# One issue order of a scheduled SSM-and-MLP kernel replaced by another

## Chip, cores and metric

The kernel runs on one core of a Trainium2 chip. The metric is the device time of one execution in microseconds; 153.26 us is the median of three runs of the kernel before (153.21 to 153.65). The engines are named as the profile names them: PE is TensorE (matmuls), PEld its weight loads, DVE is VectorE, ACT is ScalarE, POOL is GpSimd, SP is SyncE, which here only issues transfers. Each engine takes its own instructions strictly in order; between engines only semaphores order the work.

## The reference

`x` is 2048 tokens of 448 features in bf16. It is normalised, and two branches work on the result: a diagonal complex state-space model (SSM) with 448 states, and an MLP of 448 to 1792 to 448 with its own LayerNorm. The output is `x + s * silu(mlp)`.

```python
xn = _layernorm(x)
# branch A, the SSM
Lam_bar = exp(dt * (Lambda_re + 1j * Lambda_im))
B_bar   = ((Lam_bar - 1.0) / Lam)[:, None] * Bmat
h_t     = Lam_bar * h_(t-1) + B_bar @ xn_t          # for 2048 steps t
s       = 2.0 * (h @ Cmat.T).real + xn * Dskip
# branch B, the MLP
g       = silu(gelu(_layernorm(xn) @ w1 + b1) @ w2 + b2)
return x + s * g
```

## The kernel before

**Tiling.** The tokens go through in four groups g of 512: two blocks of 256, and in each block the even and the odd tokens as a tile of 128 partitions. A block's recurrence is worked for pairs of tokens, so a scan has 256 steps.

**Stages of a group.** LayerNorm statistics (DVE, L399 and L405) give a mean and a reciprocal root (the chain L478 to L488 on DVE or L478 to L482 on POOL), with which L499 (DVE) or L500 (ACT) writes the normalised x. Transfers with transposition on SP turn it into `xnT` and `xn2T`. The MLP's first matmul is L801 on PE: 14 column tiles of w1 in seven pairs, and for each pair a first phase of 6 matmuls and a second of 8, in the PSUM bank pairs (0,1), (2,3) and (4,7); the gelu with bias `b1f` is L805 on ACT. The second matmul is L828 in banks 5 and 6; DVE adds `b2bc` in L831, and the silu is L833 on ACT, or L835 on ACT with L836 on DVE. The SSM's input matmul is L729 in bank 4, copied out in L417 (`u0` to `u3`); L744 to L748 rotate it on DVE, the scans are L753 and L755 on DVE, L417 casts their result to bf16 (`sb`, 128x1536), L771 to L775 rotate back into `h`. The output matmuls L871, L874 and L877 collect in bank 7; there are four for a group, one for each block and parity. DVE reads the even ones directly in L885 (`t30_0`) or L888 and the odd ones in L883 (`xr`). L891 adds x, and a transfer stores the tile.

**The head.** Until the first weights are there, PE runs dummy matmuls (L422), transposes parameters (L529, L530) and normalised x (L460), and turns the bias b1 into columns (L602, L603), which one copy, L605, puts into `b1f`. The two loads of b1 are issued by POOL (`br0`, 3x512, and `br1`, 256 numbers), as are those of `b2bc` and `dbc` later; all loads of x and weights are SP's. The SSM's parameters are worked out in some hundred small steps on POOL, DVE and ACT (L532 to L598), among them a sine by a polynomial (L542 to L551, POOL). The matrices L712 and L697 combine B and C; their epilogues are L417 and L718, and for the last L704 and L705 on DVE (`M03`).

**What sets the order.** The kernel adds 633 tasks to a list; what each reads and writes gives the semaphore waits. The order is written out by hand in two tables. `ORDER` is one permutation of the tasks, and an engine's queue is what of it falls to that engine. Some tasks can run on either of two engines; those whose numbers stand in `SECOND` take the second.

```python
def either(self, first, second, reads=(), writes=(), prio=0.0, chain=False):
def emit(self):
    self.link()
    for k in SECOND:
        self.tasks[k].choose(1)
    order = [self.tasks[k] for k in ORDER]
```

Of the kernel before, what the change touches and what calls it, by code (L numbers as in the profile page):

```python
# [159 lines left out]


ORDER = [int(k) for k in """
# [17 lines left out]
""".split()]  # L180
SECOND = [int(k) for k in """
45 53 54 61 63 66 69 74 76 83 112 130 133 158 160 162 163 165 177 184 185 187 189 190 220 222 224 226 228 230 238 248 249 258 266 268 331 362 364 365
384 400 401 436 447 468 480 482 487 491 499 501 502 504 510 528 529 609 612 627
""".split()]


# [834 lines left out]
```

## Time and profile before

| | before |
|---|---|
| runs, median (lowest to highest) | 153.26 us (153.21 to 153.65) |
| profiled execution, span | 151.8 us |
| PE busy | 147.1 us |
| DVE busy | 127.6 us |
| ACT busy | 99.0 us |
| POOL busy | 42.1 us |

The span runs from the first instruction to the last one of the profiled execution; the time of a run is taken around the whole execution and includes some 1.5 us more. Busy time is the time in which an engine had at least one instruction in execution. A row of a timeline gives the start in us, the length in us, engine, line, operation, what is written and read and how often, and in brackets how long the engine was idle before and what ended it. In the page's slices each digit is the busy share of a fortieth of the span in tenths. A row of groups ends with busy us, mean ns of one, and the idle time ahead with its releaser; a row of waits with the us in all, the number of times and the longest.

### The profile page before, as it was taken

How to read it: one execution, taken by the hardware profiler on the slowest of the kernel's cores; microseconds unless marked ns; L12 is line 12 of the kernel's file. 1: busy time of each engine (PE TensorE's matmuls, PEld its weight loads, DVE VectorE, ACT ScalarE, POOL GpSimd, SP SyncE). 2: the span in 40 equal slices, each digit the busy share in tenths (PEclk: the TensorE clock that was granted, in tenths of full speed). 3: DMA queues.
4: the chain of work that ended last, by engine and by line, in shares of the span. 5: the costliest groups of instructions: out<-in, count | busy, mean ns of one | idle time of the engine just before them, and what ended most of it. 6: DMA issues, size and time to landing. Idle time of an engine off the chain costs nothing.

```text
span 151.8 us, 2974 instructions
## 1 busy us (share of the span) xinstructions
PE 147.1 (97%) x1127; PEld 86.6 (57%) x1127; DVE 127.6 (84%) x267; ACT 99.0 (65%) x183; POOL 42.1 (28%) x101
## 2 busy tenths in 40 slices
PE   7899999999999999999999999999999999999992
PEld 7785755454566577545444556764454666555551
DVE  2874999999978979999999996379968726999984
ACT  3888996988789559997898610463579834067400
POOL 5376827153020920010456006200072031000201
PEclk9999999999999999999999999999999999999999
DMA  4999999989997300700003032610331001100022
GB/s 116 262 305 390 266 202 138 219 152 133 165 261 180 65 0 0 138 0 4 0 0 63 4 60 45 154 60 4 60 101 23 0 4 57 64 0 0 4 84 98
DMA packets 31236, 14.73 MB, mean 97 GB/s; under 512 B 24752, under 2 KB 30774, under 8 KB 31222
## 3 DMA queue, kind: packets, MB, share of 16 engines
q1 hardware_dynamic: 30912, 14.26, 41.8%
q0 software_dynamic: 160, 0.23, 1.0%
q8 instruction: 9, 0.15, 0.4%
q10 hardware_dynamic: 150, 0.05, 0.1%
q14 instruction: 5, 0.04, 0.1%
HBM read 6.89 MB, written 1.84 MB: 57 GB/s over the span
## 4 chain that ended last, share of the span: by engine, by line
PE 80%; DVE 9%; DMA 4%; SPq 4%; issue 2%
PE psum L828 23%; PE psum L801 22%; PE psum L729 14%; PE psum L871 13%; DMA x_all<-in_A_x_dram 4%; PE psum L874 4%; SPq L84 4%; PE psum L712 3%; DVE xn_sb L499 2%; DVE lnst L399 1%; DVE s_w L628 1%; PE psum L877 1%; DVE o L831 1%; PE psum L697 1%; DVE tmp L891 1%
## 5 line engine op out<-in xcount | busy, mean ns | idle before, releaser
L801 PE MATMUL psum<-xn2T,w_sb 64*128 64x512 bf16 (+1 forms) x462 | 44.6, 345 | 0.3 <-ACT xn2T L417 0.2
L828 PE MATMUL psum<-w_sb,gT 128*128 128x448 bf16 x224 | 44.5, 353 | 0.2 <-DVE o L831 0.2
L805 ACT ACTIVATE gT<-psum,b1f 128x512 bf16<-128x512 f32 (+1 forms) x66 | 35.9, 625 | 10.4 <-PE psum L801 10.2
L801 PEld LDWEIGHTS psum<-xn2T,w_sb 64*128 64x128 bf16 x462 | 24.1, 109 | 19.8 <-ACT gT L805 2.3
L828 PEld LDWEIGHTS psum<-w_sb,gT 128*128 128x128 bf16 x224 | 21.5, 98 | 20.7 <-DVE o L831 0.6
L417 ACT ACTIVATE u_sb<-psum 128x512 bf16<-128x512 f32 (+2 forms) x22 | 10.5, 478 | 23.0 <-PE psum L729 22.7
L729 PE MATMUL psum<-xnT,BT 128*128 128x256 bf16 x196 | 24.0, 273 | 0.0
L729 PEld LDWEIGHTS psum<-xnT,BT 128*128 128x128 bf16 x196 | 18.9, 98 | 5.4 <-issue 1.1
L891 POOL TENSOR_TENSOR tmp<-t,x_all 128x448 bf16<-128x448 bf16 x5 | 5.2, 1032 | 33.1 <-DVE t L888 30.7
L753 DVE TENSOR_TENSOR_SCAN s_w<-dk,vs 128x774 f32<-128x774 f32 x8 | 14.0, 1760 | 0.1
L500 ACT ACTIVATE xn_sb<-x_all,lnw 128x448 bf16<-128x448 bf16 (+2 forms) x21 | 13.0, 662 | 1.2 <-DVE xn_sb L499 1.1
L417 ACT ACTIVATE vs<-s_w 64x256 bf16<-64x256 f32 (+2 forms) x16 | 10.9, 681 | 2.6 <-DVE s_w L753 1.5
L871 PE MATMUL psum<-CZ,h_sb 128*128 128x448 bf16 x56 | 11.9, 352 | 0.0
L871 PE MATMUL psum<-CQ,h_sb 128*128 128x448 bf16 (+2 forms) x54 | 10.5, 332 | 0.0
L399 DVE BATCH_NORM_STATS2 lnst<-x_all 128x6 f32<-128x448 bf16 x12 | 7.1, 617 | 3.4 <-DMA x_all<-in_A_x_dram 3.4
L831 DVE TENSOR_TENSOR o<-psum,b2bc 128x448 f32<-128x448 f32 x16 | 9.7, 614 | 0.2
L871 PEld LDWEIGHTS psum<-CZ,h_sb 128*128 128x128 bf16 x56 | 5.4, 98 | 4.7 <-DVE lnmv L405 0.4
L871 PEld LDWEIGHTS psum<-CQ,h_sb 128*128 128x128 bf16 x54 | 5.1, 98 | 4.0 <-DVE t L885 0.4
L874 PE MATMUL psum<-M,xnT 128*128 128x448 bf16 x32 | 7.4, 352 | 0.0
L480 POOL TENSOR_TENSOR lnw<-lnw,mhalf 128x8 f32<-128x8 f32 x3 | 7.2, 2404 | 0.3
L883 DVE TENSOR_TENSOR Cr<-psum,xd 128x448 f32<-128x448 f32 x7 | 4.3, 620 | 3.5 <-PE psum L877 3.4
L499 DVE TENSOR_SCALAR xn_sb<-x_all,lnw 128x448 bf16<-128x448 bf16 (+2 forms) x19 | 6.9, 396 | 0.0
(160 smaller groups left out, 189.1 us busy)
## 6 DMA issues: line engine op xcount, KB each, us to landing
out_dram<-tmp SPq DMA_DIRECT2D x7, 224.0 KB, 2.0
x_all<-in_A_x_dram SPq DMA_DIRECT2D x3, 448.0 KB, 4.0
w_sb<-in_B_w_dram SPq DMA_DIRECT2D x3, 448.0 KB, 8.4
w_sb<-in_B_w_dram SPq DMA_DIRECT2D x3, 384.0 KB, 4.8
vs<-in_A_C_re_dram SPq DMA_DIRECT2D x1, 392.0 KB, 11.6
Bn<-in_A_B_im_dram SPq DMA_DIRECT2D x1, 336.0 KB, 10.2
Bn<-in_A_B_re_dram SPq DMA_DIRECT2D x1, 336.0 KB, 10.5
vs<-in_A_C_im_dram SPq DMA_DIRECT2D x1, 336.0 KB, 10.8
```

The lines of the kernel that those rows point to most:

```text
L399: dve([lambda e, b=b, par=par, q=q: e.bn_stats(lnst[:, q, :], x_all[:, 2 * g + b, par, :])], [f"x{2 * g + b}"] , [f"st{q}"], 0.62, prio)
L417: kb.either(("act", [lambda e, o=o, i=i: e.activation(o, i, ACT.Copy) for o, i in pairs]), ("dve", [lambda e, o=o, i=i: e.tensor_copy(o, i ...
L499: on = [("dve", [lambda e, o=o, i=i: e.tensor_scalar(o, i, rs, nb, op0=ALU.mult, op1=ALU.add) for o, i in parts], 0.4, 0.12), ("act", [lam ...
L500: ("act", [lambda e, o=o, i=i: e.activation(o, i, ACT.Identity, bias=nb, scale=rs) for o, i in parts], 0.75, 0.2)]
L729: fns = [lambda e, r=r, m=m, d=d: e.matmul(psum[:, 4, r * NK:(r + 1) * NK], BT[:, m, d, :], xnT[:, gx, d, :], start=(d == 0), stop=(d == 6 ...
L753: dve(lambda e, so=so, vi=vi: e.tensor_tensor_scan(so, dk[:].rearrange("p i c -> p (i c)"), vi, 0.0, ALU.mult, ALU.add), ["v", "vl", "dk", ...
L801: return lambda e: e.matmul(view(bk[k]), w1_sb[rows, d, fcol(2 * j + k)], rhs[rows, d, :, :], start=not second and n == 0, stop=second and ...
L805: act([lambda e, k=k: e.activation(gT[:, gb, 2 * j + k, :].rearrange("p (r c) -> p r c", r=2)[:, :, cols], view(bk[k]), ACT.Gelu_apprx_tan ...
L828: fns = [lambda e, fi=fi: e.matmul(psum[:, bk, 0:D], gT[:, gb, fi, q * 128:(q + 1) * 128], w2_sb[:, fi, :], start=(fi == 0), stop=(fi == N ...
L831: dve(lambda e: e.tensor_tensor(o2[:, fb, :], psum[:, bk, 0:D], b2bc[:], ALU.add), [f"ps{bk}", "b2bc"], [f"oo{fb}"], 0.62, prio - 76)
L871: fns = [lambda e, k=k: e.matmul(psum[:, bk, c0:c1], h_sb[:, hb, k, k0:k0 + 128], cm[:, k, c0:c1], start=(k == 0), stop=False) for k in ra ...
L874: fns += [lambda e, d=d: e.matmul(psum[:, bk, c0:c1], xnT[:, gx, d, xs], M0[:, d, c0:c1], start=False, stop=(d == 3)) for d in range(4)]
```

## The change

Only `ORDER` and `SECOND` are replaced. No instruction's arguments change and no step is added or taken out; each of the 633 tasks is emitted once, in another place and in some cases on its other engine. The loads from memory keep their order on SP. The tables' first lines:

```diff
 ORDER = [int(k) for k in """
-0 13 19 47 9 16 18 20 14 1 94 26 17 95 91 27 92 21 15 24 48 4 96 12 108 93 90 109 97 104 103 25 105 99 22 98 49 50 55 5 51 65 106 2 110 100 111 107 29
+47 16 9 13 19 24 18 17 15 20 2 14 4 0 3 26 5 7 27 1 94 25 21 10 95 91 96 22 48 90 92 108 29 49 93 97 51 66 50 109 30 104 52 103 110 99 32 55 105 65
...
 SECOND = [int(k) for k in """
-45 53 54 61 63 66 69 74 76 83 112 130 133 158 160 162 163 165 177 184 185 187 189 190 220 222 224 226 228 230 238 248 249 258 266 268 331 362 364 365
+34 45 70 71 72 74 75 76 81 82 83 107 130 133 155 156 157 158 159 160 184 187 189 194 198 220 222 226 230 234 238 240 244 248 249 258 269 349 362 364
```

With `SECOND` some tasks change their engine. Among those that the prediction speaks of: three of the four copies of the scan's result (L417, `sb`), those of groups 0 and 1 among them, go from ACT to DVE, group 0's LayerNorm chain from POOL (L478 to L482) to DVE (L478 to L488), the magnitude step behind L626 from DVE (L631) to ACT (L630), five LayerNorm applications from ACT (L500) to DVE (L499), `b1f`'s copy L605 from DVE to ACT.

POOL at the start of the kernel, before (`dk` here is the buffer of the b1 rows, `ident`, `sgn`, `eps` are constants):

```order
L308 MEMSET ident 128x128
L327 MEMSET eps 128x1
L328 MEMSET eps 128x1
L309 ISA
L309 AFFINE_SELECT ident<-ident 128x128
L84 DMA dk<-in_B_b_dram 3x512
L326 MEMSET mhalf 128x1
L84 DMA dk<-in_B_b_dram 1x16x16
L540 TENSOR_TENSOR cw<-cw 128x4
L315 IOTA dk 128x256
```

And now:

```order
L327 MEMSET eps 128x1
L84 DMA dk<-in_B_b_dram 3x512
L311 MEMSET sgn 128x4
L328 MEMSET eps 128x1
L308 MEMSET ident 128x128
L312 ISA
L312 AFFINE_SELECT sgn<-sgn 128x1
L315 IOTA dk 128x256
L319 TENSOR_SCALAR sgn<-sgn 128x1
L309 AFFINE_SELECT ident<-ident 128x128
L84 DMA dk<-in_B_b_dram 1x16x16
```

The first b1 load moved ahead of most constants, the second behind them.

POOL around the load of `b2bc`, before (`ang` is the sine's buffer, `cw` the parameter columns):

```order
L544 TENSOR_TENSOR ang<-ang 128x16
L312 AFFINE_SELECT sgn<-sgn 128x1
L320 MEMSET sgn 128x1
L84 DMA b2bc<-in_B_b_dram 128x448
L545 TENSOR_SCALAR ang<-ang 128x16
```

And now:

```order
L551 TENSOR_TENSOR ang<-ang 128x16
L561 TENSOR_TENSOR cw<-cw,ang 128x4 x2
L561 TENSOR_TENSOR cw<-cw 128x4
L598 TENSOR_TENSOR ang<-ang,sgn 128x1
L564 TENSOR_SCALAR cw<-cw 128x4
L561 TENSOR_TENSOR cw<-cw 128x4
L564 TENSOR_SCALAR cw<-cw 128x4 x2
L561 TENSOR_TENSOR cw<-cw 128x4 x4
L564 TENSOR_SCALAR cw<-cw 128x4
L84 DMA b2bc<-in_B_b_dram 128x448
```

The load stood ahead of the sine's polynomial (from L545 on) and stands behind it and behind the parameter steps that follow it.

DVE around the first output block's L885 (`t<-psum,g_sb`), before:

```order
L836 SCALAR_TENSOR_TENSOR g_sb<-th,o 128x448
L405 BN_AGGR lnmv<-lnst 128x2
L499 TENSOR_SCALAR xn_sb<-x_all,lnw 128x448
L755 SCALAR_TENSOR_TENSOR s_w<-cw,cur,vs 128x256
L753 SCALAR_TENSOR_TENSOR s_w<-dk,vs 128x774
L885 SCALAR_TENSOR_TENSOR t<-psum,g_sb 128x448
L753 SCALAR_TENSOR_TENSOR s_w<-dk,vs 128x774
L764 TENSOR_TENSOR ang<-s_w,ang 128x16
```

And now:

```order
L836 SCALAR_TENSOR_TENSOR g_sb<-th,o 128x448
L748 TENSOR_TENSOR vs<-pa 128x256
L753 SCALAR_TENSOR_TENSOR s_w<-dk,vs 128x774
L755 SCALAR_TENSOR_TENSOR s_w<-cw,cur,vs 128x256
L753 SCALAR_TENSOR_TENSOR s_w<-dk,vs 128x774
L836 SCALAR_TENSOR_TENSOR g_sb<-th,o 128x448
L764 TENSOR_TENSOR ang<-s_w,ang 128x16
L417 CAST vs<-s_w 128x3x2x256
L885 SCALAR_TENSOR_TENSOR t<-psum,g_sb 128x448
```

Both scans (L753) of group 1, a second L836, L764 and the cast of the scans' result stand ahead of L885 now; the second scan and L764 stood behind it, and the cast was ACT's.

More of the change, by code (lines that the diff above doesn't have):

```diff
@@ L162 @@
 ORDER = [int(k) for k in """
[17 rows of a table removed]
[17 rows of a table added]
 """.split()]
 SECOND = [int(k) for k in """
-45 53 54 61 63 66 69 74 76 83 112 130 133 158 160 162 163 165 177 184 185 187 189 190 220 222 224 226 228 230 238 248 249 258 266 268 331 362 364 365
-384 400 401 436 447 468 480 482 487 491 499 501 502 504 510 528 529 609 612 627
+34 45 70 71 72 74 75 76 81 82 83 107 130 133 155 156 157 158 159 160 184 187 189 194 198 220 222 226 230 234 238 240 244 248 249 258 269 349 362 364
+397 400 401 432 440 444 446 447 449 450 468 469 480 487 501 502 504 505 507 508 512 514 525 529 530 531 572 576 589 597 627
 """.split()]
```

32 rows, old and new, of the table ORDER are left out of this document.

## The prediction

> **What bounds the kernel now.** I read the page first, its busy shares and the slices.
>
> ```profile
> span 151.8 us, 2974 instructions
> PE 147.1 (97%) x1127; PEld 86.6 (57%) x1127; DVE 127.6 (84%) x267; ACT 99.0 (65%) x183; POOL 42.1 (28%) x101
> PE   7899999999999999999999999999999999999992
> DVE  2874999999978979999999996379968726999984
> ```
>
> PE (TensorE) is busy 147.1 of 151.8 us and full in every slice but the first three and the last. So the matmuls set the time, and an order can change the time in two ways only: it closes a hole in PE, or it opens one. The second view is busy time by window.
>
> ```profile
> core 0: us, PE busy (x) PEld busy (x) DVE busy (x) ACT busy (x) POOL busy (x), PEclk, DMA share, GB/s
> 5.00:10.00 5.00, 4.57 (x77) 3.82 (x76) 3.57 (x15) 4.59 (x13) 2.64 (x10) 1.00 1.00 263
> 15.00:20.00 5.00, 4.87 (x68) 3.31 (x65) 4.66 (x20) 5.00 (x11) 4.20 (x16) 1.00 1.12 260
> 20.00:30.00 10.00, 9.82 (x52) 4.80 (x50) 9.86 (x28) 8.55 (x15) 3.16 (x8) 1.00 1.15 185
> 0.00:67.40 67.40, 65.56 (x570) 41.30 (x570) 57.65 (x149) 54.95 (x105) 24.68 (x76) 1.00 0.78 168
> 67.40:80.40 13.00, 13.00 (x111) 6.18 (x109) 12.86 (x25) 10.83 (x21) 4.97 (x8) 1.00 0.00 1
> 80.40:100.00 19.60, 19.60 (x124) 11.67 (x121) 14.88 (x28) 8.73 (x15) 5.29 (x8) 1.00 0.32 63
> ```
>
> Holes still to be closed are small: 0.43 us in 5 to 10, 0.13 in 15 to 20, 0.18 in 20 to 30, none from 67.4 on until 100. Holes to be opened are what matters, and the same rows name the engine: from 67.4 to 80.4 DVE (VectorE) is busy 12.86 of 13.00 us, and before that 57.65 of 67.4. How close it runs to PE there is in the timelines of both.
>
> ```profile
> 77.44 1.49 PE L871 MATMUL psum<-CZ,h_sb 128*128 128x448 bf16 x7
> 79.62 1.06 PE L801 MATMUL psum<-xn2T,w_sb 64*128 64x512 bf16 x8
> 80.61 1.31 PE L871 MATMUL psum<-CQ,h_sb 128*128 128x448 bf16 x6
> 66.25 0.61 DVE L836 SCALAR_TENSOR_TENSOR g_sb<-th,o 128x448 bf16<-128x448 f32 x1
> 66.78 0.61 DVE L705 TENSOR_TENSOR M<-psum,tmp 64x448 bf16<-64x448 f32 x1
> 78.05 1.75 DVE L753 TENSOR_TENSOR_SCAN s_w<-dk,vs 128x774 f32<-128x774 f32 x1
> 79.73 0.62 DVE L885 SCALAR_TENSOR_TENSOR t<-psum,g_sb 128x448 bf16<-128x448 f32 x1
> 80.27 1.76 DVE L753 TENSOR_TENSOR_SCAN s_w<-dk,vs 128x774 f32<-128x774 f32 x1
> ```
>
> All L871 groups of these stretches write PSUM bank 7. The group at 80.61 cannot start before DVE's L885 has read the group before it (t30_0 in the code), and L885 ends at 79.73 + 0.62 = 80.35, 0.26 us ahead. Some 0.1 to 0.15 of that is the handing over, so DVE has next to no slack at this point. Ahead of 80.61 the new order gives PE the same matmuls as the old one. So whatever makes L885 late makes the whole rest late.
>
> **The change, part by part. DVE ahead of L885.** The change moves tasks between DVE, ACT and POOL and puts later work of DVE in front of L885. I compare the two DVE orders up to that instruction. A step costs what lies between one start and the next (L836 at 66.25, L705 at 66.78: 0.53 for an instruction of 0.61, since the ends overlap). Prices not seen yet:
>
> ```profile
> 17.65 0.16 DVE L478 TENSOR_SCALAR lnw<-lnmv 128x4 f32<-128x4 f32 x1
> 19.92 0.17 DVE L488 SCALAR_TENSOR_TENSOR lnw<-lnmv,lnw 128x8 f32<-128x8 f32 x1
> L626 DVE TENSOR_SCALAR s_w<-s_w 128x1024 f32<-128x1024 f32 x1 | 0.7, 694 | 0.0
> L631 DVE SCALAR_TENSOR_TENSOR s_w<-s_w 128x1024 f32<-128x1024 f32 x1 | 1.2, 1226 | 0.0
> L417 ACT ACTIVATE vs<-s_w 128x1536 bf16<-128x1536 f32 x4 | 5.9, 1487 | 1.6 <-DVE s_w L753 1.5
> L499 DVE TENSOR_SCALAR xn_sb<-x_all,lnw 128x448 bf16<-128x448 bf16 x7 | 2.7, 387 | 0.0
> ```
>
> Newly ahead of L885: the LayerNorm chain of group 0 (L478 to L488, POOL before), 2.3 by the first two rows; one scan L753, 1.8; one L831 and two L836, 3 x 0.53 = 1.6; two copies of the scan's result (L417, 128x1536, ACT before), see below; five L499 of 448 from ACT, 5 x 0.31 = 1.55, and four pieces of 384 and 128, 1.2; nine parameter steps of 0.15, 1.35; a transposed x copy, 0.4; L764, 0.1. Without the copies 10.3. No longer ahead of it: L631 1.15, two PSUM copies 1.2, three L499 0.9, one L848 0.3, a weight copy 0.3, L605 0.2, seven small ones 0.55: 4.6. Four L659 come and four go, which I take as even.
>
> The two L417 copies have no DVE row. As one source and f32 in SBUF they are nearest to L626: 694 x 1536/1024 = 1.04 each. The bounds are 0.9 (448 elements of L499 in 0.31 give 1.06, less fixed cost) and 1.84 (L631, which has an f32 source at half that rate). I take 1.0, so 2.0 for both, bounds 1.8 and 3.7. The Trainium skill, VectorE: DVE Perf Modes, section Mode 2×_2P, gives a copy from SBUF to SBUF two results a cycle, which at its 0.96 GHz is an estimate of 0.8 each, 0.4 less in the sum below; no row of this trace has such a copy.
>
> The sum is 10.3 + 2.0 - 4.6 = 7.7 us more DVE work ahead of L885. What takes it up is the time in which DVE waits, by the view of waits:
>
> ```profile
> DVE lnst L399 <- DMA x_all<-in_A_x_dram: 3.4, 3, 2.0
> DVE pa L744 <- ACT u_sb L417: 2.0, 2, 1.5
> DVE lnst L431 <- DMA x_all<-in_A_x_dram: 1.8, 1, 1.8
> DVE w_sb L352 <- DMA w_sb<-in_B_w_dram: 1.0, 1, 1.0
> DVE dk L323 <- PEq L1006: 0.9, 1, 0.9
> ```
>
> Up to 80.35 DVE is busy 57.65 + 12.86 = 70.5 us, so 9.85 are free. The new work makes 70.5 + 7.7 = 78.2. Of the free time, 2.7 can't be filled (L323 and L431: nothing to do before the first x has landed). The L399 wait is filled by the LayerNorm chain, now ahead of L399, and the one for u goes when DVE is behind. That puts L885's end at 80.9 at the least. I add 0.8 for gaps between short dependent instructions, which the old order had too, and 0.7 for a remaining wait in the head (DVE's L624 now follows a longer POOL chain). L885 ends at 82.4, bounds 80.9 and 84, against 80.35. PE's L871 then starts near 82.65 in place of 80.61: **+2.0 us**. As a cross-check, L705, 13 us earlier, releases PE's L801 in the old order 0.84 us before it is wanted; by the same difference of work it comes some 2.5 later, which opens the first 1.6 of the hole there already.
>
> **The head.** The second b1 load moves behind seven POOL instructions.
>
> ```profile
> 0.79 0.20 POOL L308 MEMSET ident<- 128x128 bf16 x1 [0.29 <-POOLq L1006]
> 1.50 0.80 POOL L84 DMA_DIRECT2D dk<-in_B_b_dram  x1
> 2.33 0.54 POOL L84 DMA_DIRECT2D dk<-in_B_b_dram  x1
> 5.63 0.34 POOL L315 IOTA dk<- 128x256 f32 x1
> 6.34 0.27 PE L602 MATMUL psum<-ident,dk 4*128 4x3 bf16 x4 [0.15 <-DMA dk<-in_B_b_dram]
> 6.85 2.39 PE L801 MATMUL psum<-xn2T,w_sb 64*128 64x256 bf16 x40 [0.19 <-ACT xn2T L417]
> dk<-in_B_b_dram POOLq DMA_DIRECT2D x1, 3.0 KB, 3.2
> dk<-in_B_b_dram POOLq DMA_DIRECT2D x1, 0.5 KB, 3.9
> ```
>
> The first b1 load can start at about 1.1 (it waits for one DVE memset) and takes 0.8; then come three memsets, two affine selects, the iota of 0.34 and a small multiply, 1.5 together by rows like L308 and L315. So the second is issued near 3.4, not 2.33. It lands 3.9 later, 7.3 (3.2 by the first load's row: 6.6). L602, which in the old order waited for it until 6.34, comes to 7.4, and L801, behind it on PE, to 7.8: +0.95, bounds +0.2 and +1.5. ACT's table load for the gelu goes behind the b1 copy now and moves by the same. This is a hole in the head, but it is no addition to the 2.0: PE that is late by 0.95 simply waits that much less for L885.
>
> **PE's own order.** Six L828 go between the L801 groups, and group 1's L801 run in one piece. The most this can bring is the holes of the three windows above less the hole at L602 and L801, some 0.5, and about 0.2 for a change of mode saved. I take -0.6 together (bounds 0 and -0.9). PE's own arrival at L871 would be 80.61 + 0.95 - 0.6 = 80.95, well ahead of 82.65. It too is swallowed.
>
> **After 100 us** the work is the same, DVE has 4.7 us free between 80.4 and 100, and its work from L885 to the last rotations is some 2.4 less than before, what was brought forward. I take 0, bounds -0.2 and +0.5.
>
> Sum: 151.8 + 2.0 + 0 = 153.8 us of span. The runs' median, 153.26, is 1.46 above the profiled span, so 155.3 us.
>
> **The rivals.** *Same time (head only).* DVE finds room after all, L885 ends by 80.8, and only 0.95 - 0.6 = +0.35 is left: 153.6, within half a us of no change. For it: 9.85 us free against 7.7 added. Against it: 2.7 of the free time is before the first x. *Faster (PE's holes close).* The place is the head: b1 lands at 6.6, as fast after its issue as the first load, so L801 starts at 7.1 (+0.25), and the holes and mode changes up to 31 us give 0.9 back: 152.6. It decides only if L885 also ends before 80.2, that is, if DVE's added work is below 7.0 and nothing but the first 2.7 is waited for. *Slower still (b2).* The load of b2bc moves behind the whole parameter chain on POOL.
>
> ```profile
> b2bc<-in_B_b_dram POOLq DMA_DIRECT2D x1, 112.0 KB, 7.0
> dbc<-in_A_Dskip_dram POOLq DMA_DIRECT2D x1, 112.0 KB, 4.6
> ```
>
> It was issued at about 13.6 and is now some 13 POOL instructions of 0.25 behind the sine chain's end (about 13.5), and two of these wait for DVE: 17 to 18.5. Landing 7.0 later is 24 to 25.5, and DVE's first L831, which needs it, is due at about 25. If it is late, DVE stands with all its queue behind it, up to 1.3 more at L885: 156.6. At 4.6 it costs nothing. That the change does not do what its words say is part of every case: a stretch of about 1 us in which PE waits at L602 is new.
>
> **How the numbers follow.** Forecast 155.3, own range 154.0 to 156.2: 0.55. Slower still, 156.6: 0.20. Same, 153.6: 0.12. Faster, 152.6: 0.13. The range that leaves out 2 in 10 goes from 153.0 to 157.0. A difference under 0.3%, 0.46 us, is not told from none here: faster (below 152.8) 0.14, the third case and a tail of the second; same 0.12, the second case; slower 0.74, the rest of the two others.
>
> **What would show it.** DVE's L885 of the first output block ending near 82.4, with PE's L871 behind it waiting "<-DVE t L885", and a hole of 1 to 2 us on PE between 67 and 83, where now there is none. L602 near 7.4 and the first L801 near 7.8. DVE's busy time up by about 7 us, ACT's down. The prediction is wrong if PE has no hole there, or if DVE's copies take less than 0.9; then the head's part decides and the time is near 153.5 or below. If the hole is at L828 near 25 us, the b2 load was it.

## The result, and the profile after

| | before | after |
|---|---|---|
| runs, median (lowest to highest) | 153.37 us (153.21 to 153.65) | 155.07 us (154.63 to 156.43) |
| ratio of after to before | | 1.0126, interval 1.0082 to 1.017 |
| spans of these runs | | 152.7, 152.9, 153.3, 154.4 us |
| span of the profiled execution | 151.8 us | 152.7 us |
| PE / DVE / ACT / POOL busy | 147.1 / 127.6 / 99.0 / 42.1 us | 147.1 / 130.5 / 96.0 / 35.1 us |

The new order is 1.7 us slower, between 0.8% and 1.7%. The forecast was 155.3. The number fits and the reason does not. The ratios here and below leave out an execution that lies more than 1.5% above the fastest of its kernel (156.84 of e34 and 157.48 of b1 among them); the medians hold all. After's profiled execution took 154.63, 1.9 us more than its span; executions of the kernel before with a span of 151.8 took 153.5 to 153.6 in the experiments below, some 1.75 more. So the spans can be compared, within 0.2 us.

The page of after, its span, its busy times and the rows of PE and the granted clock in slices:

```profile
span 152.7 us, 2979 instructions
PE 147.1 (96%) x1127; PEld 87.5 (57%) x1127; DVE 130.5 (85%) x281; ACT 96.0 (63%) x184; POOL 35.1 (23%) x91
PE   7699999999999999999999999999999999999992
PEclk9999999999999999999999999999999999999999
```

PE does the same 147.1 us in all, so the difference of the spans is again time in which PE stands. The view by window, in four of the prediction's stretches, the last one moved on by the 1.0 us that after is behind there:

```profile
core 0: us, PE busy (x) PEld busy (x) DVE busy (x) ACT busy (x) POOL busy (x), PEclk, DMA share, GB/s
5.00:10.00 5.00, 3.69 (x61) 3.08 (x60) 4.62 (x17) 3.66 (x12) 3.54 (x18) 1.00 0.97 269
15.00:20.00 5.00, 5.00 (x70) 3.71 (x68) 4.79 (x21) 4.17 (x10) 3.28 (x12) 1.00 1.13 257
20.00:30.00 10.00, 10.00 (x64) 5.20 (x58) 9.48 (x29) 9.64 (x17) 0.16 (x1) 1.00 0.88 171
68.40:81.40 13.00, 13.00 (x110) 6.79 (x109) 12.58 (x22) 11.92 (x23) 2.35 (x1) 1.00 0.11 21
```

From 68.4 to 81.4, where the prediction had its hole of 2 us, PE is busy 13.00 of 13.00 us. That is the prediction's own sign of being wrong; its consequence there, a time near 153.5, did not come either. The hole stands in the head instead (3.69 in 5 to 10, before 4.57), while the stretch from 15 to 30 is now full, which before had 0.31 us free. PE's waits, its timeline at the places where it is behind, and DVE's timeline at L885:

```profile
PE psum L602 <- DMA dk<-in_B_b_dram: 1.1, 1, 1.1
PE psum L729 <- ACT u_sb L417: 0.3, 1, 0.3
PE psum L460 <- DVE xn_sb L453: 0.3, 1, 0.3
PE psum L801 <- ACT gT L805: 0.2, 1, 0.2
```

```profile
7.30 0.27 PE L602 MATMUL psum<-ident,dk 4*128 4x3 bf16 x4 [1.05 <-DMA dk<-in_B_b_dram]
7.55 2.05 PE L801 MATMUL psum<-xn2T,w_sb 64*128 64x256 bf16 x34
...
30.16 5.36 PE L801 MATMUL psum<-xn2T,w_sb 64*128 64x512 bf16 x48
35.74 1.05 PE L801 MATMUL psum<-xn2T,w_sb 64*128 64x512 bf16 x8 [0.23 <-ACT gT L805]
62.35 1.70 PE L729 MATMUL psum<-xnT,BT 128*128 128x256 bf16 x14 [0.31 <-ACT u_sb L417]
78.44 1.49 PE L871 MATMUL psum<-CZ,h_sb 128*128 128x448 bf16 x7
81.61 1.31 PE L871 MATMUL psum<-CQ,h_sb 128*128 128x448 bf16 x6
```

```profile
79.14 1.21 DVE L417 CAST vs<-s_w 128x1536 bf16<-128x1536 f32 x1
80.73 0.62 DVE L885 SCALAR_TENSOR_TENSOR t<-psum,g_sb 128x448 bf16<-128x448 f32 x1 [0.38 <-PE psum L874]
```

L885 ends at 81.35 and the L871 that needs its bank starts at 81.61, the same distance of 0.26 as before. But L885 itself had waited 0.38 us for PE's L874. PE is late here and DVE with it; both of PE's L871 are 1.00 behind (77.44 and 80.61 before). The delay arose earlier, and piece by piece. At 30 us almost nothing of it is there; the L801 that starts in before at

```profile
30.08 7.26 PE L801 MATMUL psum<-xn2T,w_sb 64*128 64x512 bf16 x64
```

starts at 30.16. The head lost 0.70 us (first L801 at 7.55, not 6.85), and by 30 us 0.6 of it is won back. The rest comes behind that. PE's stretch from this L801 to the L871 that needs L885's bank, of before and then of after:

```profile
30.08:80.61 50.53, 50.53 (x390) 28.56 (x390) 47.37 (x99) 41.26 (x75) 13.89 (x29) 1.00 0.44 83
```

```profile
30.16:81.61 51.45, 50.91 (x390) 29.13 (x390) 49.55 (x96) 46.00 (x88) 11.71 (x22) 1.00 0.49 94
```

After takes 0.92 us longer for the same 390 matmuls. 0.54 of it are the two waits, at 35.74 for the gelu and at 62.35 for `u1`. The other 0.38 is no idle time in this view: the matmuls lie further apart, and their overlapping ends hide short waits (at 68.83, where L705 is still reading a bank, a pair of L801 is followed after 304 ns and not 213). 0.19 of it is in the group of 90 L801 that starts at 68.38 (10.06 us to the next group, before 9.87).

So in the one profiled execution some 0.9 us are to be explained. The median is 1.7 behind. The remainder is in what differs between executions: after's spans run from 152.7 to 154.4, while 45 of the 63 executions of the kernel before that stand beside the experiments lie between 151.4 and 151.8.

### The profile page after: what moved, and what is told of

Read it like the earlier page. It is cut to its first block, busy times and chain, and to the rows that moved or that the text cites. A ratio compares the mean times of both kernels' runs of the same rounds, so it can differ in the third digit from the quotient of the medians.

```text
span 152.7 us, 2979 instructions
## 1 busy us (share of the span) xinstructions
PE 147.1 (96%) x1127; PEld 87.5 (57%) x1127; DVE 130.5 (85%) x281; ACT 96.0 (63%) x184; POOL 35.1 (23%) x91
## 4 chain that ended last, share of the span: by engine, by line
PE 69%; ACT 8%; DMA 7%; DVE 7%; POOL 5%; issue 3%; ACTq 0%; POOLq 0%; DVEq 0%
PE psum L828 19%; PE psum L801 18%; PE psum L871 13%; PE psum L729 12%; DMA b2bc<-in_B_b_dram 5%; PE psum L874 4%; DMA dk<-in_B_b_dram 2%; ACT gT L805 2%; DVE Bn L661 1%; DVE o L831 1%; ACT xn_sb L500 1%; ACT u_sb L417 1%; DVE tmp L659 1%; POOL cw L561 1%; PE psum L877 1%
## 5 line engine op out<-in xcount | busy, mean ns | idle before, releaser
L801 PE MATMUL psum<-xn2T,w_sb 64*128 64x512 bf16 (+1 forms) x462 | 44.5, 345 | 0.2 <-ACT gT L805 0.2
L828 PE MATMUL psum<-w_sb,gT 128*128 128x448 bf16 x224 | 44.4, 353 | 0.0
L801 PEld LDWEIGHTS psum<-xn2T,w_sb 64*128 64x128 bf16 x462 | 25.0, 109 | 19.0 <-ACT gT L805 3.1
L828 PEld LDWEIGHTS psum<-w_sb,gT 128*128 128x128 bf16 x224 | 21.6, 98 | 19.9 <-issue 0.8
L729 PE MATMUL psum<-xnT,BT 128*128 128x256 bf16 x196 | 24.0, 273 | 0.3 <-ACT u_sb L417 0.3
L729 PEld LDWEIGHTS psum<-xnT,BT 128*128 128x128 bf16 x196 | 18.8, 98 | 6.1 <-issue 1.1
L417 ACT ACTIVATE u_sb<-psum 128x512 bf16<-128x512 f32 (+2 forms) x20 | 9.3, 464 | 16.9 <-PE psum L729 16.6
L500 ACT ACTIVATE xn_sb<-x_all,lnw 128x448 bf16<-128x448 bf16 (+2 forms) x23 | 14.1, 655 | 3.3 <-DVE xd L848 3.2
L753 DVE TENSOR_TENSOR_SCAN s_w<-dk,vs 128x774 f32<-128x774 f32 x8 | 13.9, 1753 | 0.0
L831 DVE TENSOR_TENSOR o<-psum,b2bc 128x448 f32<-128x448 f32 x16 | 9.8, 614 | 4.2 <-PE psum L828 3.9
L871 PE MATMUL psum<-CZ,h_sb 128*128 128x448 bf16 x56 | 11.9, 353 | 0.0
L871 PE MATMUL psum<-CQ,h_sb 128*128 128x448 bf16 (+2 forms) x54 | 10.5, 332 | 0.0
L835 ACT ACTIVATE th<-o 128x448 f32<-128x448 f32 x8 | 4.6, 574 | 7.3 <-DVE o L831 7.2
L417 ACT ACTIVATE vs<-s_w 64x256 bf16<-64x256 f32 (+2 forms) x13 | 6.5, 496 | 3.6 <-DVE s_w L753 3.4
L871 PEld LDWEIGHTS psum<-CZ,h_sb 128*128 128x128 bf16 x56 | 5.4, 98 | 4.7 <-issue 0.4
L871 PEld LDWEIGHTS psum<-CQ,h_sb 128*128 128x128 bf16 x54 | 5.1, 98 | 4.0 <-DVE cur L765 0.4
L874 PE MATMUL psum<-M,xnT 128*128 128x448 bf16 x32 | 7.4, 352 | 0.0
L836 DVE SCALAR_TENSOR_TENSOR g_sb<-th,o 128x448 bf16<-128x448 f32 x8 | 5.8, 728 | 1.7 <-ACT th L835 1.7
L833 ACT ACTIVATE g_sb<-o 128x448 bf16<-128x448 f32 x8 | 4.4, 568 | 4.6 <-DVE o L831 4.5
```

The lines of the kernel that those rows point to most:

```text
L417: kb.either(("act", [lambda e, o=o, i=i: e.activation(o, i, ACT.Copy) for o, i in pairs]), ("dve", [lambda e, o=o, i=i: e.tensor_copy(o, i ...
L500: ("act", [lambda e, o=o, i=i: e.activation(o, i, ACT.Identity, bias=nb, scale=rs) for o, i in parts], 0.75, 0.2)]
L729: fns = [lambda e, r=r, m=m, d=d: e.matmul(psum[:, 4, r * NK:(r + 1) * NK], BT[:, m, d, :], xnT[:, gx, d, :], start=(d == 0), stop=(d == 6 ...
L753: dve(lambda e, so=so, vi=vi: e.tensor_tensor_scan(so, dk[:].rearrange("p i c -> p (i c)"), vi, 0.0, ALU.mult, ALU.add), ["v", "vl", "dk", ...
L801: return lambda e: e.matmul(view(bk[k]), w1_sb[rows, d, fcol(2 * j + k)], rhs[rows, d, :, :], start=not second and n == 0, stop=second and ...
L828: fns = [lambda e, fi=fi: e.matmul(psum[:, bk, 0:D], gT[:, gb, fi, q * 128:(q + 1) * 128], w2_sb[:, fi, :], start=(fi == 0), stop=(fi == N ...
```

## The experiments

Twelve kernels on three chips, each beside the kernel before (medians 153.28, 153.42 and 153.40 there). In the edits a number is a task: 24 and 25 are the two loads of b1, 43 the load of `b2bc`, 111 is L602 and L603, 112 L605, 363 L705, 384 the copy of `u1`, 449 an application L500. `ORDER` and `SECOND` are those of the changed kernel, for e2 those of the kernel before.

### The change again, and the head

**a0** is the changed kernel on another chip, in five rounds.

> The changed order once more, to have its spread and a second profile beside the others. Theory (call it M03): DVE's L705 comes 1.6 us later than before (ends 69.0, before 67.4), and the second group of six L801 of token group 2, which needs its bank, starts 0.9 later; all that PE loses earlier (b1 at L602, the gelu table, the copy of u1) is swallowed by that one wait. Rival (head): the late b1 load is what is passed on. Rival (L885): the first output block's L885. All three expect the same here: 154.6 to 156.4 us, median near 155.1, with L602 waiting about 1 us and a hole of about 0.1 before the third L801 pair near 69.

Median 156.12, ratio 1.0155 (1.0112 to 1.0197). Four of its five executions had a granted clock of 0.988 to 0.989 and spans of 153.9 to 155.2; the fifth 1.0 and 153.1. The profiled one was the slowest; its timeline and its clock by window:

```profile
8.23 0.27 PE L602 MATMUL psum<-ident,dk 4*128 4x3 bf16 x4 [1.98 <-DMA dk<-in_B_b_dram]
...
8.48 3.23 PE L801 MATMUL psum<-xn2T,w_sb 64*128 64x256 bf16 x34
...
32.66 3.63 PE L801 MATMUL psum<-xn2T,w_sb 64*128 64x512 bf16 x32
```

```profile
core 0: us, PE busy (x) PEld busy (x) DVE busy (x) ACT busy (x) POOL busy (x), PEclk, DMA share, GB/s
6.25:8.23 1.98, 0.00 (x1) 0.03 (x1) 1.63 (x8) 0.50 (x2) 1.61 (x6) 1.00 0.88 246
8.23:9.17 0.94, 0.94 (x19) 0.89 (x21) 0.91 (x4) 0.56 (x2) 0.15 (x1) 1.00 0.95 298
9.18:12.59 3.41, 3.41 (x34) 2.31 (x28) 1.09 (x4) 2.74 (x6) 1.61 (x8) 0.50 0.99 318
12.59:16.00 3.41, 3.41 (x49) 2.48 (x49) 3.04 (x18) 2.41 (x6) 1.78 (x8) 1.00 1.01 371
```

The same load, issued at the same 3.63, landed 4.5 us later here and 3.5 in the first profile, so PE stood for 1.98 us and not 1.05. One microsecond after it had started again, the granted clock fell to 0.50 for 3.41 us. The first 34 L801 took 3.23 us, not 2.05. At 30 us a0 is 2.5 behind the first profile of the same kernel: 0.93 by the later landing, some 1.57 by the clock. Half speed over 3.41 us is 1.7 lost of 155.2, or 1.1%: that is the mean clock of 0.989 which the list of executions shows. Nothing behind wins this back. In the stretch of the same length ahead, 5.76 to 9.17, PE is busy 1.43 us of 3.41. In the first profile the clock's record begins at 4.78, the stretch from there to 8.19 holds 2.10 us of PE's work, and the next one is granted 1.00. So where the pause falls in such a stretch may decide; with one profile of the low clock this is a lead and not shown.

The Trainium skill, TensorE: Matmul & The Clock Gate, section HAM oscillation — how this bites in real kernels, gives the rule that PE should have no idle gap over some 3.4 us. Here a gap of 1.98 us, without any work of PE's, was followed by the half clock, and the measurement decides; the 3.41 us at half clock have the length of the window that the page gives, 3.4 us.

**e1** puts the second b1 load directly behind the first, **e34** moves two steps later in the program, **e134** does both.

```diff
e1:  +ORDER.remove(25); ORDER.insert(ORDER.index(24) + 1, 25)
e34: +ORDER.remove(363); ORDER.insert(ORDER.index(362) + 1, 363)
     +ORDER.remove(449); ORDER.insert(ORDER.index(384) + 1, 449)
```

> The second b1 load is issued directly behind the first, all else as in the changed order. M03: L602 no longer waits, the first L801 starts near 6.9 in place of 7.55, but L705 still ends near 69.0, so the time falls by 0 to 0.3 us, to about 154.9. Head: the 0.7 us come back whole, 154.4 or below. L885: as M03, no gain.

> L705 directly behind L704 on DVE (two instructions of 1.3 us no longer ahead of it), and the copy of u1 on ACT ahead of one L500. M03: L705 ends near 67.7, the hole before the L729 at 62.3 (0.3) closes, PE comes 0.4 to 0.6 earlier to the group-2 L801 and finds the bank free: 154.5 to 154.7. Head: these two places cost nothing, 155.1. L885: PE gains there and loses it at 80.6, where DVE had 0.4 us of waiting left: no more than 0.4 gained, 154.7.

> Both edits together. M03: with L705 out of the way the earlier head counts: 0.8 to 1.2 less than the changed order, 153.9 to 154.3, near the kernel before. Head: as with the b1 load alone, 154.4. L885: 0.4 at most, 154.7, and a wait for DVE's L885 before the L871 at about 81.

| | median | ratio (interval) | spans at clock 1.0 | clock about 0.989 |
|---|---|---|---|---|
| e1 | 154.8 | 1.0089 (1.0053 to 1.0124) | 152.4 to 153.3 | 0 of 6 |
| e34 | 154.8 | 1.0096 (1.0065 to 1.0127) | 152.0 to 153.5 | 4 of 12 |
| e134 | 154.72 | 1.0084 (1.0051 to 1.0117) | 152.4 to 152.9 | 1 of 6 |

e1 took the wait at L602 away and made a new one, since the constants now stand behind both loads:

```profile
4.26 0.23 PE L529 MATMUL psum<-ident,dk 3*128 3x3 bf16 x3 [0.50 <-POOL ident L309]
6.57 0.42 PE L422 MATMUL psum<-const-bfloat16-1.0 128*128 128x128 bf16 x2
7.38 2.70 PE L801 MATMUL psum<-xn2T,w_sb 64*128 64x256 bf16 x34
```

Its L801 start hardly earlier and run at half pace until 8.8: their pairs start 214 ns apart and then 109. The half pace was there before the L801 began. In after the same two dummy matmuls take

```profile
5.97 0.28 PE L422 MATMUL psum<-const-bfloat16-1.0 128*128 128x128 bf16 x2
```

In every trace the first dummy matmuls start some 107 ns apart. In after they come to some 55 at about 5 us, where its record of the clock begins (4.78); in e1 they stay at 107 until the L801. e1's trace holds no record of the clock at all, and the view then gives 1.00; so a late start at full pace does not show in an execution's mean clock. e1's profile is 0.49 behind after at 30 us (30.65) and at the last matmul (150.08). None of its executions shows the low clock. e34 keeps after's head (L801 at 7.55), has no hole at L729, and PE is ahead by what was expected (0.4 to 0.6):

```profile
61.88 1.69 PE L729 MATMUL psum<-xnT,BT 128*128 128x256 bf16 x14
77.96 1.49 PE L871 MATMUL psum<-CZ,h_sb 128*128 128x448 bf16 x7
81.12 1.12 PE L871 MATMUL psum<-CQ,h_sb 128*128 128x448 bf16 x5
```

0.48 and 0.49 ahead of after, and 0.49 at the last matmul (149.10, 149.59): in the profiles the place of `u1`'s copy and of L705 costs half a microsecond. How it divides between the two was not tested. Among the executions at clock 1.0 the spans' median is 152.5 in e34 and 152.9 in after. Both edits together, e134, are no better in the median than either alone (its head has e1's half pace too, until about 8.1); the medians, which hold the executions with the low clock, don't tell the three apart.

### POOL's head in the old order, and the old kernel with the late load

**h1** gives POOL's first six steps the order of the kernel before; **h2** is h1 and e34 in one; **e2** is the kernel before with four constants ahead of its second b1 load, the opposite test.

```diff
h1: +for k in (25, 24, 1, 14, 13, 0):
    +    ORDER.remove(k); ORDER.insert(3, k)
e2: +for k in (2, 3, 5, 7):
    +    ORDER.remove(k); ORDER.insert(ORDER.index(25), k)
```

> The changed order with POOL's first six tasks as in the kernel before: ident first, then both b1 loads, then the constants. Theory (head): PE's wait at L602 (1.05 us in one profile, 1.98 in another) and the low clock that follows it are most of the loss. So the first L801 starts near 6.9, no execution but a rare one has a clock of 0.989, and the median falls from 155.1 to 156.1 to 153.7 to 154.2, 0.2 to 0.7 above before, the rest being the holes before 70 us. Rival (M03, the bank of L705): what is gained in the head is waited for near 69 us, 154.7 or more in executions of full clock. Rival (L885): DVE's added work shows as soon as PE is early, a wait for L885 at 81 and 154.5.

> The same head, and L705 directly behind L704 and u1's copy ahead of one L500. Head and holes together: 0.4 to 0.5 less than with the head alone, 153.2 to 153.7, level with the kernel before. L885: no gain over the head alone, DVE's L885 late.

> The kernel before with four constants of POOL put ahead of its second b1 load, which is so issued about 1 us later; nothing else changed. Head: L602 waits 0.9 to 1 us more, the first L801 starts at 7.6 to 7.9, and some or most executions lose the clock behind it: 153.9 to 154.5 where the clock stays, 155 to 156 where it doesn't, median 154.0 to 155.5. M03 and L885: these place the loss later, in the order of DVE, which here is the old one: no more than 0.3 slower, 153.6.

| | median | ratio (interval) | spans at clock 1.0 | clock about 0.989 |
|---|---|---|---|---|
| h1 | 154.48 | 1.0075 (1.0045 to 1.0105) | 152.1 to 153.2 | 3 of 12 |
| h2 | 154.4 | 1.005 (1.0015 to 1.0084) | 151.6 to 153.4 | 1 of 12 |
| e2 | 153.71 | 1.0038 (0.9997 to 1.0079) | 151.8 to 152.1 | 4 of 12 |

h1 has no wait at L602 and reaches the L801 of after's 30.16 at 29.65; at its last matmul 0.31 of the 0.51 is left (149.28, 149.59), since it waits 0.32 for the gelu at 35.44. It is not the load of b1 alone: h3 (below) has the same early load and is at 30.11 there, because a piece of w1 came later. h1's median missed the forecast of 153.7 to 154.2, and three of its twelve executions have the low clock, though its profile has no wait at L602.

e2 shows the two parts by themselves. PE waits 0.95 us at L602; eight of the twelve executions have spans of 151.8 to 152.1, with 151.9 in the middle, where the kernel before beside them has 151.7 and so 0.2 less, and four have the low clock and are 1.5 us longer again (153.4 to 154.1). In the profile the last matmul is 0.15 later (148.81, 148.66). So at full clock the wait costs less than the 153.9 to 154.5 that the head's theory gave; the rivals' 153.6 is nearer. Of the 29 executions of the kernel before, beside them on that chip, two had the low clock. The interval of the ratio touches 1, so in the medians alone this is no result.

h2 was to be level with the kernel before. Its fastest executions are (151.6), but they spread over 2 us, and its profile shows why:

```profile
24.05 0.62 DVE L831 TENSOR_TENSOR o<-psum,b2bc 128x448 f32<-128x448 f32 x1 [1.06 <-DMA b2bc<-in_B_b_dram]
```

```profile
24.82 5.46 PE L828 MATMUL psum<-w_sb,gT 128*128 128x448 bf16 x28 [0.37 <-DVE o L831]
```

This is the prediction's rival about `b2bc`. The load was issued at 15.78 and landed 8.2 us later; DVE's first L831 stood 1.06 for it, PE's L828 0.37 for DVE.

### DVE's load

**h5** is h1 with two of the three casts of the scan's result back on ACT.

```diff
+SECOND.remove(349); SECOND.remove(397)
```

> The changed order with the old head of POOL, and two of the three copies of the scan's result (groups 0 and 1) back on ACT: 2.4 us less on DVE ahead of L885. L885 (the prediction's step): if that load is what binds, 0.5 to 1 us less than with the head alone. Head and holes: DVE already waits for PE at L885, so no gain; within 0.3 of the head alone, or slower, since ACT gets 3 us of copies between the others of 60 to 80 us.

Median 156.37, ratio 1.0167 (1.0124 to 1.0211), 1.9 us slower than h1. DVE is indeed freed, and L885 shows it:

```profile
80.90 0.62 DVE L885 SCALAR_TENSOR_TENSOR t<-psum,g_sb 128x448 bf16<-128x448 f32 x1 [1.50 <-PE psum L874]
```

```profile
PE psum L729 <- ACT u_sb L417: 1.0, 2, 0.6
...
PE psum L828 <- ACT gT L805: 0.8, 1, 0.8
```

DVE waits 1.50 for PE, and PE now waits for ACT, on which the casts (1.48 us each) stand ahead of `u`'s copies and the gelu. In h1 the same L885 waits 0.37 for PE. So DVE's added work is not what binds at L885; with two of the casts back, ACT binds.

### What is left

**b1** (the name of this kernel, not of the bias) issues `b2bc` earlier and nothing else; **c1** covers the wait for the bias with PE's own work; **h3** is h2 with the earlier `b2bc`; **c3** is c1, e34 and the earlier `b2bc`.

```diff
b1: +for k, at in ((43, 69),): ORDER.remove(k); ORDER.insert(ORDER.index(at) + 1, k)
c1: +for k, at in ((111, 113), (102, 111), (112, 102), (117, 118),): ORDER.remove(k); ORDER.insert(ORDER.index(at) + 1, k)
```

> The changed kernel with one move: POOL issues the load of b2bc directly behind the first L564 that follows the sine (at about 13.6 us) and no longer behind the parameter steps (15.97). Theory (the late load of b2bc costs between 0 and 1 us, because it lands between 23.6 and 24.1 while DVE's first L831 wants it at 23.0 to 23.2): it lands at 20.5 to 22, L831 no longer waits for it, PE's L828 behind it neither; median 0.2 to 0.6 us below the changed kernel's 155.1, most of it from executions in which the load landed late, so about 154.6. Rival (the landing is covered in nearly every execution, as in the profile of the changed kernel): the wait of 0.38 goes from the row of L831 and the median stays within 0.2 of 155.1.

> The changed kernel with PE's first 12 matmuls of L801 ahead of L602, the gelu's table load ahead of the copy L605, and one pair's first phase (L801 into bank 4) behind the next second phase, so that PE does not stand still for the late load of b1; the loads stay as they are. Theory (the wait for b1 costs 0.4 to 0.6 us by itself and more through the granted clock that falls after it): L801 starts at 6.6 to 6.9 instead of 7.55, L602 has no wait over 0.3, the executions with a granted clock of about 0.989 become no more frequent than in the kernel before (4 of 46), and the median falls by 0.5 to 1.2 us against the changed kernel, to 154.0 to 154.6. Rival (the clock has nothing to do with this wait): L602's wait goes, the median falls by 0.3 to 0.5, and about half of the executions stay at 0.989. Second rival (the gelu and its table load set the pace of the head): PE waits as long at the third pair of L801 and the median stays.

> The changed kernel with POOL's first steps in the order of the kernel before (both loads of b1 early), L705 directly behind L704, one LayerNorm application L500 behind the copy of u1, and b2bc issued behind the first L564 after the sine. The same without the last of these had a median of 154.4 and a profile in which L831 waited 1.06 for b2bc. Theory (b1, b2bc, L705 and u1's copy are all that costs more than 0.2 us): span 151.4 to 151.9, median 153.3 to 153.8, level with the kernel before within 0.3%. Rival (something further in the order costs half a us or more, such as the gelu's table load or DVE's load before L885): median 154.0 or more, with no wait of L831 for b2bc.

> The changed kernel with the twelve matmuls of L801 ahead of L602 and the table load ahead of L605, L705 directly behind L704, the L500 behind the copy of u1, and b2bc issued behind the first L564 after the sine. Theory: the loads of b1 stay late and cost nothing; median 153.2 to 153.9, level with h3 and with the kernel before, and if the earlier table load also brings the first gelu ahead, below 153.2. Rival (the head is bound by something else, so that the moved matmuls only move the wait): 154.3 or more, with a new wait of PE for the gelu of the first pairs.

| | median | ratio (interval) | spans at clock 1.0 | clock about 0.989 |
|---|---|---|---|---|
| b1 | 155.6 | 1.0115 (1.008 to 1.015) | 152.6 to 155.5 | 2 of 6 |
| c1 | 154.97 | 1.0098 (1.0075 to 1.0122) | 152.6 to 153.7 | 0 of 6 |
| h3 | 154.05 | 1.0045 (1.0016 to 1.0074) | 151.5 to 153.3 | 2 of 12 |
| c3 | 154.56 | 1.0102 (1.0062 to 1.0141) | 152.1 to 152.6 | 2 of 6 |

b1: the load landed at 21.2 and L831 no longer waits, and the median did not fall; it is nearer to the rival, whose 155.1 it is 0.5 above. In its profile the L801 that waits for the gelu starts at 35.64, in after at 35.74, and the last matmul is 0.11 earlier. So the late landing is not quite covered in after: the chain that ended last runs from its landing at 23.5 over DVE's work and the gelu to that L801. It costs 0.1 us there, and more with an earlier head, as in h2.

c1 is the miss that taught most. The wait at L602 is gone, and the next stage is reached at the same time all the same. In c1:

```profile
6.91 1.06 PE L801 MATMUL psum<-xn2T,w_sb 64*128 64x256 bf16 x12 [0.64 <-ACT lnw L438]
7.91 0.30 PE L602 MATMUL psum<-ident,dk 4*128 4x3 bf16 x4
...
9.49 0.62 PE L460 MATMUL psum<-ident,xn_sb 128*128 128x128 bf16 x8
```

In h3, with the early load of the bias:

```profile
6.85 0.52 PE L801 MATMUL psum<-xn2T,w_sb 64*128 64x256 bf16 x6 [0.28 <-DVE xn2T L417]
7.84 1.71 PE L801 MATMUL psum<-xn2T,w_sb 64*128 64x256 bf16 x28 [0.47 <-DMA w_sb<-in_B_w_dram]
9.48 0.62 PE L460 MATMUL psum<-ident,xn_sb 128*128 128x128 bf16 x8
```

After itself reaches this L460 at 9.53. The x for the first L801 comes at 6.8, and behind six matmuls the next piece of w1 is waited for, until 7.84 in h3. In h1's profile that piece came earlier and L460 started at 9.03. So behind the late b1 stands another load that sets the head in some executions, and filling the first hole alone brings 0.04 in that profile. In c1 itself the seventh of the twelve matmuls starts at 7.47, 0.30 after the sixth; the profile names no wait for it, so that it was the same piece is inferred. For the profile the second rival of c1 holds (PE waits elsewhere), though for the weights and not for the gelu. The median, 154.97, is 0.1 below after's first four runs and 1.15 below a0's on another chip: none of c1's six executions had the low clock, and those at clock 1.0 are no shorter than after's. That would fit the clock as what the wait costs, but c3, with the same cover, had it in two of six.

c3's median is 0.7 above its forecast and in its rival's range, but the wait for the gelu of the first pairs which that rival named is not there.

h3 has the best median of the variants of the changed kernel, 154.05, 0.65 above the kernel before beside it (153.40). Its rival's figure (154.0 or more, no wait of L831 for `b2bc`) is what came. At the last matmul its profile is 0.56 ahead of after and 0.37 behind the kernel before (149.03; 149.59 and 148.66). Part of it can be seen: in h3 PE's L801 at 35.68 waits 0.22 for the gelu, as in after, and the head waits 0.47 for w1. None of the twelve kernels is faster than the kernel before.

## Why the prediction was right in the number and wrong in the reason

- **"DVE ahead of L885 ... +2.0 us": wrong, and the step that failed is the sum of DVE's added work.** It had 7.7 us more ahead of L885. The windows up to L885's start, the first of before and the second of after, measure it:

```profile
0.00:79.73 79.73, 77.89 (x673) 47.21 (x675) 69.84 (x172) 65.36 (x125) 28.98 (x84) 1.00 0.66 143
```

```profile
0.00:80.73 80.73, 78.04 (x673) 48.20 (x675) 74.34 (x188) 69.62 (x138) 25.85 (x81) 1.00 0.65 147
```

  The third busy time is DVE's: 4.5 us more, and its free time fell from 9.9 to 6.4. The casts were priced about right (1.0; the row is 1.21 with a pitch of 1.14, and the estimate of 0.8 by the Trainium skill, VectorE: DVE Perf Modes, section Mode 2×_2P, is further off). Three others were priced too high. The LayerNorm chain, priced 2.3, is ten instructions of 0.16 to 0.21, some 1.8, and the chain that before has too took 0.4 less in one step (L483: 0.55, then 0.20). Four L499 came on balance (13 before, 17 after) and not six: 1.2, not 1.85. The small parameter steps add 0.3 on balance, not 0.8. These three make some 2 of the 3.2 us; the rest is spread over small differences and overlapping ends. And the prediction left DVE 4.2 us of free time up to L885's end; after has 6.4 and L885 is not late by itself. It waited 0.38 for PE, and in h5, with two casts less, 1.50.
- **The cross-check at L705: half right.** L705 ends at 68.99 and not 67.39, 1.6 later:

```profile
68.38 0.61 DVE L705 TENSOR_TENSOR M<-psum,tmp 64x448 bf16<-64x448 f32 x1
```

  PE is 0.8 later there itself (its L801 at 68.38, 67.57 before), and the hole that I put at 1.6 is under 0.1. Together with `u1`'s copy, which I did not look at, the two places cost 0.49 in the profile (e34).
- **The head: the landing right, "swallowed" wrong.** The second load was issued at 3.63 (3.4 forecast), landed near 7.2 (7.3), L602 came at 7.30 (7.4), the first L801 at 7.55 (7.8). But there was no L885 to swallow the delay. a0's 2.5 us were passed on whole; the late load by itself costs some 0.2 us at full clock in the old order (e2), and 1.5 more where the clock falls. The clock was in no step of the sum.
- **PE's own order, -0.6: right in the sum, open in the cause.** The head lost 0.70 at 7.55 and 0.08 at 30 us. But e2, in the old order, also wins 0.36 of its 0.50 back by then (first L801 at 7.35, the L801 of 30.08 at 30.22); and h1, whose first L801 is level with before's (6.79, 6.85), is 0.43 ahead at 30 us, h3 with 6.85 is 0.03 behind. What the order alone brings lies between. "After 100 us 0": right, 1.00 behind at 81.6 and 0.93 at the last matmul (149.59, 148.66 before).
- **What lies outside the span** was taken as 1.46, from the median of the runs over the profiled span. Executions with that span of 151.8 take 1.75 more. With 1.75 the same sum would have said 155.55.
- **The rivals.** *Head only*, 153.6, had the mechanism nearest to what happened; it was too low because the head's loss includes the clock and because the waits for `u1`, L705 and the gelu were left out. *b2* is real as a mechanism (h2: 1.06), and in after worth 0.1. *Faster* asked for b1 to land at 6.6; in the two profiles of the changed order it landed near 7.2 and 8.1.

So the agreement of 155.3 with 155.07 is luck: a hole of 2 us that did not open stands in place of several small losses. In the profiles, at the last matmul, after is 0.93 behind; `u1` and L705 alone give back 0.49 of it (e34), POOL's old head alone 0.31 (h1), the earlier `b2bc` alone 0.11 (b1), and the three together 0.56 and not 0.91 (h3). The rest of the median is what differs between executions, with some 1.5 us where the clock falls. **What stays open:** the 0.37 that h3 keeps. Between 30 and 81 us h3 falls 0.4 behind the kernel before (30.11 to 81.06, before 30.08 to 80.61), of which the 0.22 at the gelu has a row and the rest is matmuls lying further apart. That gelu is late because the table load L618 ahead of it starts 0.39 us after the silu that it follows; in the kernel before it started 0.08 after a silu that ended at the same time, and nothing in the profile says why:

```profile
31.89 1.28 ACT L618 ACT_TABLE_LOAD   x1 [0.39 <-ACT g_sb L833]
```

And whether the clock falls in an execution was seen in a profile once; that the wait at L602 brings it on rests on the counts: 15 of 39 executions of the kernels with that wait at L602 (after, a0, e2, e34, b1), 10 of 66 of the variants without it or with it covered, 5 of 63 of the kernel before. On each of the three chips of the experiments the share is the higher with the wait (8 of 17 against 1 of 12, 4 of 12 against 5 of 30, 2 of 6 against 4 of 24). But c3, with the wait covered, has 2 of 6 and h1, whose profile is without it, 3 of 12, so the wait is not the whole of it; and since a trace without a record of the clock counts as 1.00, as e1's does, the counts can be too low. The link to the wait is argued and not shown.

## What to carry to other kernels

A new order is judged where PE waits, engine by engine, with the issue times of the small loads looked up first: a load of 512 bytes, issued 1.3 us later, was followed in one profile by a pause of 1.98 us and a stretch at half clock, while 4.5 us of work added to DVE did not hold PE up at L885. Work added to an engine that is 84% busy is not a delay until the free time ahead of the waiting instruction is used up; count the instructions on balance, type by type, and price chains by their rows and not by the time from their first to their last. When one hole in the head is closed, look at which load lands next before expecting the gain. And undo several parts together as well as one by one: here the single gains did not add up.

## What the runs showed of the hardware that was not expected

A pause of 1.98 us on PE was followed, 0.94 us after work had begun again, by 3.41 us at a granted clock of 0.50 (a0), and such an execution has a mean clock of 0.989; in the first profile, a pause of 1.05 us was followed by none. The same POOL load of 512 bytes, issued at 3.63 in both, landed 3.5 and 4.5 us later, and `b2bc` took from 6.1 to 8.2 us. PE begins every trace at half pace (dummy matmuls 107 ns apart) and goes over to full pace (some 55) at about 5 us in after and at 8.8 us in e1; in e1 the view gave a clock of 1.00 from a trace without any record of it.
